# VectorE's order between the ranking and the second expert written out, and two GpSimd drains

## The chip, the cores and the metric

The kernel runs on one core of one Trainium2 chip. The metric is the device time of one execution in microseconds (us); the kernel before has a median of 478.66 us over three runs. In the profile TensorE is PE (its weight loads PEld), VectorE is DVE, ScalarE is ACT, GpSimd is POOL and SyncE is SP. A name with a q behind it (POOLq, SPq) is that engine's instruction queue: waits, register work, DMA issues, drains.

## The reference

Two stages follow each other. The first is block-sparse attention; the second sends each token of its output through one of eight experts, at most 80 tokens for each.

```python
# attention: q, k, v are (4, 8, 768, 64); blocks of 32; a row sees its neighbours,
# the first and the last block, and three sampled blocks
attn = softmax(where(mask, q @ k.T / 8, -1e9));  x = (attn @ v) as (3072, 512)
# experts: w_gate (512, 8), w1 (8, 512, 1024), w2 (8, 1024, 512), capacity 80
logits = x @ w_gate;  expert_idx = argmax(logits);  gate_w = softmax(logits)[expert_idx]
for e in range(8):
    tok_idx = the (at most) 80 tokens of expert e with the largest gate_w
    out[tok_idx] = gate_w[tok_idx, None] * (relu(x[tok_idx] @ w1[e]) @ w2[e])   # other rows stay 0
```

## The kernel before

**Attention** (0 to about 343 us of the profile) works through 24 groups: a block of 128 query rows of one batch, all heads. For each group DVE, ACT and POOL copy the visible keys together (`kx`, L237 on POOL), PE makes products (L363), transposes (L383) and the sums over values (L397). Each group has eight steps; `at(d, f)` queues `f` for d steps later. PE and SP follow this order as written; the other engines are ordered by the framework's planner, from its own estimates of durations. POOL also issues DMAs of its own: 32 loads of the first and last value blocks (`vw`, `vd`, L234), all in groups 0 to 13; later eight gathers of tokens and eight scatters of results. The last part of attention counts, for each token, how many of its expert's tokens rank above it; the ranking ends with `R` (L850) on DVE.

**The experts** start with `sl` (PE, L853), which turns the ranking into lists of token numbers and gates. DVE makes `toki`, the token numbers, from it (L858), and POOL gathers the tokens' rows, expert by expert (`xg`, L871). For expert e:

- `divide(e)`: DVE adds to the softmax sums and inverts them (`rs`, L925, L927); the rows are scaled into `xd` (L934), on DVE for e < 2 and on POOL from there on.
- `turn(e)`: PE transposes `xd` into `tx` (L944); `split_ps` cuts it into a high half on ACT (`xh`, L917) and a rest on DVE (`xl`, L918).
- `first_layer(e)`: 24 PE matmuls with w1 (`ph`, L958); `relu(e)` on ACT; `turn_h(e)` transposes and splits the result (`tq`, `hh`, `hl`); `second_layer(e)`: 24 matmuls with w2 (`po`, or `ph` for the last expert, L991); `finish(e)`: DVE multiplies by the gate (`ob`, L997) and POOL scatters the rows (L998).

Weights are float32 and are multiplied as two parts. Each expert has eight blocks of 128x1024 (four of w1, four of w2), loaded by SP (`raw`, L886) into a ring of 12 buffers. ACT casts a block into its high part (L895, L904) and DVE, or POOL for the fourth block of w2 of some experts, subtracts it for the rest (the `whl` rows of L896 and L911). I call this subtraction a **sub**. The parts lie in a ring of 11 pairs. SP issues its loads in order; a load waits until both cast and sub of the block that its buffer held are done, and so do all loads behind it.

Outside of attention the planner orders PE too. An order can be forced: what is traced inside `with tc.issue_after(ins)` stands behind `ins` if it runs on the same engine. In the kernel before a few such edges hold DVE: one sub of w1[0] behind the ranking, two behind `count_rounds`, the fourth behind `divide(0)`, and the subs of w1[1] and w2[0], `divide(e)` and `turn(e)` of later experts behind `xl` of the first; among these the planner chooses. The first expert's eight blocks are called w1[0] and w2[0] here, the second's w1[1] and w2[1].

After the last scatter all engines load a round count (L1057), skip a loop over further rounds (L1058) and end in a block of drains and barriers (L1114).

Of the kernel before, what the change touches and what calls it, by code (L numbers as in the profile page):

```python
# [24 lines left out]
P = 128  # L25
# [8 lines left out]
GATED, GLATE = range(0, 6), 4  # L34
NRQ = 4
BANKS = {(22, 4): "s", (23, 2): "t", (23, 3): "s", (23, 4): "t"}
SW1, SW2 = ("vvvp", "v"), ("v", "vvvp")
NEARLY = 2
FMID = 4
GACT = (23,)  # L40
NACC = {19: 2, 20: 2, 21: 2, 22: 4, 23: 3}
# [35 lines left out]
def kernel(  # L77
# [61 lines left out]
    with ExitStack() as actx:  # L139
# [427 lines left out]
        def at(delay, fn):  # L567
            queue.setdefault(stepno[0] + delay, []).append(fn)
# [143 lines left out]
        with tc.manual_schedule(engines={ENG.PE, ENG.SP}):  # L712

            def run(fs):
                for f in fs:
                    f()

            k0, k1 = load_k(0), load_k(1)
            run(k0[:1])
            load_full(0, k0[1:] + [lambda: load_q(0)])  # L720
            run(k1)
            load_rows(0)
            run(load_v(0))
            load_q(1)
            load_rows(1)
            load_q(2)
            nc.sync.dma_start(wg, w_gate.rearrange("(c p) e -> p c e", p=P))
            load_own()

            def globals_of(pair, b):  # L730
                with tc.issue_after(order["p"]):
                    load_v_global(pair % 2, b)

            for n, (j, b) in enumerate(ORDER):
                if n == 0:
# [12 lines left out]
                if n in FLOAD:  # L748
                    at(4, lambda n=n: load_full(FLOAD[n]))
                at(5, lambda n=n: load_q(n + 3))  # L750
                if n == 10:
                    at(0, lambda: run(load_k(2)))
                    at(6, lambda: run(load_k(3)))
                if n and n % 2 == 0 and n + 2 < len(ORDER):
                    def next_v(pair=n // 2 + 1):
                        run(load_v(pair))
                        load_rows(pair + 1)
                    at(6, next_v)
                    at(3, lambda pair=n // 2 + 1: spread_mask(pair))
# [72 lines left out]
    def moe_round(first):  # L832
        def after(ins):
            return tc.issue_after(ins) if first else nullcontext()
# [18 lines left out]
                mm = nc.tensor.matmul(sl[0:SLOT, 0:48], lhsT=R[:, :, t], rhs=tab[:, t].rearrange("p a e -> p (a e)"),  # L853
                                      start=(t == 0), stop=(t == NTILE - 1))
        warm(mm.ins, NWARM[1])
        toki = mp.tile([P, 2, NE], U32, name="toki")
        with nc.allow_low_precision(reason="sums of two whole numbers, each summed up in float32 before"):
            got = nc.vector.tensor_reduce(out=toki[0:SLOT, 0, :],  # L858
                                          in_=sl[0:SLOT, 0:2 * NE].rearrange("p (a e) -> p e a", a=2), axis=AX.X,
                                          op=ALU.add)  # L860
        sv = mp.tile([P, 6, NE], F32, name="sv")
        nc.vector.tensor_copy(sv[0:SLOT].rearrange("p a e -> p (a e)"), sl[0:SLOT, 0:48])
        tok = mp.tile([P, 2, NE], F32, name="tok")
        gate = mp.tile([P, NE], F32, name="gate")
        nc.vector.tensor_add(tok[0:SLOT, 0, :], sv[0:SLOT, 0, :], sv[0:SLOT, 1, :])
# [9 lines left out]
        for e in range(NG):  # L875
            gather(e)

        def load_w(e):
            if e >= NE:
# [28 lines left out]
        def split_lo(raw, done, ins):  # L908
            with after(ins):
                for t, (hi, lo) in zip(raw, done):  # L910
                    ins = nc.vector.tensor_sub(lo, t, hi.bitcast(F32))  # L911
            return ins.ins

        def split_ps(ps, name):
            hi = hpool.tile([P, ps.shape[-1]], F32R, name=name + "h")
# [79 lines left out]
        def finish(e):  # L995
            ob = hpool.tile([P, DM], F32, name="ob")
            nc.vector.tensor_scalar(ob[0:SLOT], outs[e][0:SLOT, :], gate[0:SLOT, e:e + 1], None, op0=ALU.mult)  # L997
            nc.gpsimd.indirect_dma_start(out=out[:, :],  # L998
                                         out_offset=bass.IndirectOffsetOnAxis(ap=toki[0:SLOT, 1, e:e + 1], axis=0),
                                         in_=ob[0:SLOT, :], in_offset=None, bounds_check=NT - 1, oob_is_err=False)  # L1000

        load_w(0)
        load_w(1)

        with after(order["act"]):
            w1h[0] = split_hi(w1s[0])
        split_lo(w1s[0][:1], w1h[0][:1], ranked.ins)
        nc.vector.tensor_scalar(tok[0:SLOT, 1, :], sv[0:SLOT, 5, :], -65536.0, 65536.0, op0=ALU.mult, op1=ALU.add)
        nc.vector.tensor_add(tok[0:SLOT, 1, :], tok[0:SLOT, 1, :], tok[0:SLOT, 0, :])
        nc.vector.tensor_copy(toki[0:SLOT, 1, :], tok[0:SLOT, 1, :])  # L1010
# [1 line left out]
        nc.vector.tensor_add(gate[0:SLOT], gate[0:SLOT], sv[0:SLOT, 4, :])  # L1012
        if first:
            with after(got.ins):
                counted = count_rounds()

        split_lo(w1s[0][1:3], w1h[0][1:3], counted.ins if first else None)
        for e in range(NE + 1):
            if e == 0:
                div = divide(0)  # L1020
                split_lo(w1s[0][3:], w1h[0][3:], div.ins)
                turned = turn(0)
                split0 = order["split"]
                warm(turned.ins, NWARM[2])
                if first:
                    with after(split0), after(order["hi"]):
                        w1h[1] = split_w(w1s[1][:NEARLY], SW1[0])
            if e + 1 < NE:
                with after(split0):
                    divide(e + 1)  # L1030
                turn(e + 1)
            if 0 < e < NE:
                turn_h(e - 1)
            if e < NE:
                first_layer(e)
            if e > 0:
                with after(order["act"]) if e == 1 else nullcontext(), after(split0) if e == 1 else nullcontext():
                    w2h[e - 1] = split_w(w2s[e - 1], SW2[min(e - 1, 1)])
# [8 lines left out]
            if e + 1 < NE:  # L1047
                if e == 0:
                    with after(order["act"]), after(split0):
                        w1h[1] = w1h.get(1, []) + split_w(w1s[1][len(w1h.get(1, [])):], SW1[0])  # L1050
                else:
                    w1h[e + 1] = split_w(w1s[e + 1], SW1[1])
            if e > 0:
                finish(e - 1)

# [62 lines left out]
```

## Time and profile before

| what | us |
|---|---|
| median of three runs (lowest, highest) | 478.66 (476.11, 479.69) |
| the profiled execution, its own time | 474.34 |
| its span in the trace | 472.5 |
| PE busy / DVE busy / ACT busy / POOL busy | 382.1 / 349.8 / 310.8 / 164.0 |

The time lies 1.84 us above the span. Instructions of the queues (waits, drains, DMA issues) are not counted as busy. The page's chain of waits shares the span out as PE 38%, DVE 20%, issue 13%, ACT 12%, DMA 11% and POOL 3%.

### The profile page before, as it was taken

Reading aid. Unit: us, or ns where it says so; the run is one execution under the profiler, and the core shown is the slowest. Engines: PE = TensorE matmul, PEld = TensorE weight load, DVE = VectorE, ACT = ScalarE, POOL = GpSimd, SP = SyncE. Lnnn points to the kernel's source line nnn. Section 1 sums busy time; section 2 is a strip of 40 time slices with the busy share of each in tenths; the row PEclk is TensorE's granted clock in tenths of the full one; section 3 lists DMA queues with packets and bytes.
Section 4 is the critical chain, followed back from the end, with each engine's and each line's share of the span. In section 5 each row is a group of like instructions: output and inputs, shape, how many; then the busy total and the mean of one; then the engine's idle time right before and its main releaser. Section 6 shows DMA issues by size and latency. Waiting matters only on the chain.

```text
span 472.5 us, 16982 instructions
## 1 busy us (share of the span) xinstructions
PE 382.1 (81%) x6294; PEld 266.7 (56%) x6296; DVE 349.8 (74%) x1366; ACT 310.8 (66%) x718; POOL 164.0 (35%) x422
## 2 busy tenths in 40 slices
PE   5826878798888889897988798867497999999990
PEld 2524655476666657675766576645364656665560
DVE  3752576687678798977999878757967899988920
ACT  2542677688568796786877656876755776787810
POOL 4540133243126363433333213141244354434320
PEclk9987899889999999999999998988558899999996
DMA  8999494979219999978669747892969695999400
GB/s 302 303 300 261 127 236 134 248 252 249 71 53 271 361 296 280 259 208 237 186 173 295 206 114 194 241 285 98 402 211 292 219 341 183 333 411 409 181 16 19
DMA packets 60779, 109.35 MB, mean 231 GB/s; under 512 B 6731, under 2 KB 19020, under 8 KB 60690
## 3 DMA queue, kind: packets, MB, share of 16 engines
q1 hardware_dynamic: 58130, 101.49, 69.1%
q0 software_dynamic: 2560, 6.71, 4.9%
q8 instruction: 52, 0.85, 0.8%
q14 instruction: 37, 0.30, 0.2%
HBM read 94.38 MB, written 13.99 MB: 229 GB/s over the span
## 4 chain that ended last, share of the span: by engine, by line
PE 38%; DVE 20%; issue 13%; ACT 12%; DMA 11%; POOL 3%; SPq 1%; ACTq 0%; DVEq 0%; POOLq 0%
PE S L363 9%; PE xb L397 7%; ACT sb L375 5%; PE ph L958 5%; DVE whl L896 4%; DVE dump L537 4%; PE pt L383 3%; DVE sb L371 3%; PE Sf L654 3%; DMA raw<-in_w_dram 3%; DMA vd<-in_v_dram 3%; DMA vw<-in_v_dram 2%; PE po L991 2%; ACT xs L598 2%; PE xb L674 1%
## 5 line engine op out<-in xcount | busy, mean ns | idle before, releaser
L375 ACT ACTIVATE sb<-sb,mn 128x256 f32<-128x256 f32 (+1 forms) x192 | 90.1, 503 | 42.0 <-DVE mn L371 39.1
L371 DVE CUSTOM_DVE_ANT_0 sb<-S,mask 128x256 f32<-128x256 f32 (+1 forms) x192 | 76.9, 422 | 50.0 <-PE S L363 36.3
L363 PE MATMUL S<-kx,qt 64*32 64x256 f32 x1408 | 71.1, 410 | 27.8 <-DMA qt<-in_qn_dram 8.7
L896 DVE TENSOR_TENSOR whl<-raw,whl 128x1024 fp32r<-128x1024 f32 x53 | 73.8, 1437 | 4.5 <-ACT whl L895 4.3
L363 PEld LDWEIGHTS S<-kx,qt 64*32 64x32 f32 x1408 | 37.4, 140 | 46.3 <-issue 27.1
L237 POOL COPY kx<-kt 128x128 f32 x88 | 30.4, 464 | 95.2 <-PE S L363 92.0
L895 ACT CAST whl<-raw 128x1024 fp32r<-128x1024 f32 x60 | 59.2, 1045 | 5.3 <-DMA raw<-in_w_dram 2.8
L397 PE MATMUL xb<-vw,pts 128*32 128x65 f32 x1408 | 53.7, 231 | 8.6 <-ACT pts L349 5.3
L397 PE MATMUL xb<-vd,pts 128*32 128x65 f32 x1408 | 53.8, 227 | 4.4 <-issue 4.2
L383 PE MATMUL pt<-ident,sb 128*128 128x128 f32 (+1 forms) x384 | 51.0, 277 | 4.2 <-ACT pts L349 3.4
L397 PEld LDWEIGHTS xb<-vw,pts 128*32 128x32 f32 x1408 | 37.5, 114 | 19.6 <-ACT pts L349 9.1
L958 PE MATMUL ph<-whl,xh 128*80 128x512 f32 x128 | 43.5, 410 | 3.6 <-DVE whl L896 3.5
L383 PEld LDWEIGHTS pt<-ident,sb 128*128 128x128 f32 (+1 forms) x384 | 41.1, 146 | 7.6 <-ACT pts L349 3.6
L397 PEld LDWEIGHTS xb<-vd,pts 128*32 128x32 f32 x1408 | 41.5, 114 | 5.3 <-issue 5.2
L285 ACT COPY kx<-kt 128x128 f32 x88 | 31.4, 438 | 10.3 <-PE S L363 10.3
L991 PE MATMUL po<-whl,hh 128*80 128x512 f32 x112 | 36.5, 395 | 0.0
L537 DVE TENSOR_SCALAR_CACHE_REDUCE dump<-keyrow,keycol,cnt 128x640 bf16<-128x640 f32 (+5 forms) x36 | 32.5, 904 | 1.1
L351 DVE COPY pts<-pt 128x512 f32<-128x512 f32 (+1 forms) x48 | 30.7, 640 | 3.5 <-PE pt L383 2.7
L661 ACT ACTIVATE sbf<-sbf,mn 128x768 f32<-128x768 f32 x16 | 15.0, 936 | 24.0 <-DVE mn L660 23.4
L285 DVE COPY kx<-kt 128x128 f32 x88 | 24.6, 315 | 8.0 <-PE S L363 7.9
L654 PE MATMUL Sf<-kt,qfull 128*128 128x512 f32 (+1 forms) x64 | 26.6, 540 | 4.8 <-DMA qfull<-in_qf_dram 3.3
L598 ACT COPY xs<-xb 128x260 f32<-128x260 f32 (+2 forms) x64 | 23.4, 366 | 10.5 <-PE xb L397 10.0
(211 smaller groups left out, 778.0 us busy)
## 6 DMA issues: line engine op xcount, KB each, us to landing
raw<-in_w_dram SPq DMA_DIRECT2D x64, 512.0 KB, 7.1
vw<-in_v_dram SPq DMA_DIRECT2D x44, 390.0 KB, 7.2
vd<-in_v_dram SPq DMA_DIRECT2D x132, 130.0 KB, 5.0
vf<-in_v_dram SPq DMA_DIRECT2D x24, 260.0 KB, 5.8
x_dram<-xs SPq DMA_DIRECT2D x24, 260.0 KB, 4.4
kt<-in_kT_dram SPq DMA_DIRECT2D x8, 768.0 KB, 7.2
qt<-in_qn_dram SPq DMA_DIRECT2D x24, 256.0 KB, 3.0
out_dram<-zero SPq DMA_DIRECT2D x12, 512.0 KB, 6.2
```

Source lines behind the costliest of these rows:

```text
L285: eng(far_keys(t, hps, k, r), KT[b][:, hps, bass.ds(vals[qbs[k], r] * BLK, BLK)])
L363: nc.tensor.matmul(banks[h][BLK * k:BLK * k + BLK, i].rearrange("p (g a) c -> p g (a c)", g=2), lhsT=QT[b, j][d, hp, :, k], rhs=keys, star ...
L371: ins = nc.vector.tensor_tensor_reduce(out=sb, in0=st, in1=masks[n // 2 % 2][0:r].rearrange("p g (a c) -> p (g a) c", a=4), scale=-0.125, ...
L375: order["s"] = nc.scalar.activation(p, p, AF.Exp, bias=mn, scale=-1.0).ins
L383: nc.tensor.transpose(pt[:, (2 * i + c) * r:(2 * i + c + 1) * r], p[:, c * P:(c + 1) * P], ident[0:r, 0:r])
L397: nc.tensor.matmul(xb[place:place + 32, o:o + 65], lhsT=pts[:, c * r + BLK * k:c * r + BLK * k + BLK], rhs=(vw, vd)[c][s][:, k, xb_b, hd * ...
L537: cmp = nc.vector.tensor_scalar(d, keyrow[:, lo * P:hi * P], key, c, op0=ALU.is_le, op1=ALU.add, accum_out=c)
L654: nc.tensor.matmul(st, lhsT=q[:, hp, :], rhs=KT[b][:, hp, part], start=True, stop=True)
L895: nc.scalar.copy(hi, t)
L896: eng.tensor_sub(lo, t, hi.bitcast(F32))
L958: nc.tensor.matmul(ps[0:SLOT, :], lhsT=l[:, cs], rhs=r[:, ws], start=(i == 0), stop=(i == 3 * HP - 1))
L991: nc.tensor.matmul(po[0:SLOT, :], lhsT=l[:, cs], rhs=r[:, ws], start=(i == 0), stop=(i == 23))
```

## The change

DVE's order from the ranking to the subs of w2[0] is written out, by a chain of edges (`order["dve"]`): three subs of w1[0]; `toki` and the small operations on lists and gates up to `count_rounds`; the fourth sub of w1[0] and the first of w1[1]; `divide(0)`; the second sub of w1[1]; `xl` of expert 0; the third sub of w1[1]; `divide(1)`; the fourth; `xl` of expert 1; three subs of w2[0]; from there on the planner chooses again. ACT casts w1[0], w1[1] and three blocks of w2[0] in one go. The gathers are traced behind the first three subs. The second part adds two drains on POOL: one in group 16 of attention, behind the last `kx` copy traced until then, and one behind the scatter of expert 5, the sixth.

```diff
-SW1, SW2 = ("vvvp", "v"), ("v", "vvvp")
-NEARLY = 2
+SW1, SW2 = "v", "vvvp"
+DRAINED = (16, 5)
...
                 at(5, lambda n=n: load_q(n + 3))
+                if n == DRAINED[0]:
+                    def drained():
+                        with tc.issue_after(order["p"]):
+                            nc.gpsimd.drain()
+                    at(6, drained)
...
+            if e == DRAINED[1]:
+                with tc.issue_after(put.ins):
+                    nc.gpsimd.drain()
...
+        order["dve"] = ranked.ins
         with after(order["act"]):
-            w1h[0] = split_hi(w1s[0])
-        split_lo(w1s[0][:1], w1h[0][:1], ranked.ins)
+            w1h[0], w1h[1], w2h[0] = split_hi(w1s[0]), split_hi(w1s[1]), split_hi(w2s[0][:3])
+        split_lo(w1s[0][:3], w1h[0][:3])
+        # toki, sv, tok and the gathers stand here now
...
-                counted = count_rounds()
-
-        split_lo(w1s[0][1:3], w1h[0][1:3], counted.ins if first else None)
+                order["dve"] = count_rounds().ins
+
+        split_lo(w1s[0][3:], w1h[0][3:])
+        split_lo(w1s[1][:1], w1h[1][:1])
         for e in range(NE + 1):
             if e == 0:
-                div = divide(0)
-                split_lo(w1s[0][3:], w1h[0][3:], div.ins)
-                turned = turn(0)
-                split0 = order["split"]
+                with after(order["dve"]):
+                    order["dve"] = divide(0).ins
+                split_lo(w1s[1][1:2], w1h[1][1:2])
+                with after(order["dve"]):
+                    turned = turn(0)
+                order["dve"] = order["split"]
                 warm(turned.ins, NWARM[2])
-                if first:
-                    with after(split0), after(order["hi"]):
-                        w1h[1] = split_w(w1s[1][:NEARLY], SW1[0])
+                split_lo(w1s[1][2:3], w1h[1][2:3])
             if e + 1 < NE:
-                with after(split0):
-                    divide(e + 1)
-                turn(e + 1)
+                with after(order["dve"]) if e < 2 else nullcontext():
+                    ins = divide(e + 1).ins
+                if e == 0:
+                    order["dve"] = ins
+                    split_lo(w1s[1][3:], w1h[1][3:])
+                with after(order["dve"]) if e == 0 else nullcontext():
+                    turn(e + 1)
+                if e == 0:
+                    order["dve"] = order["split"]
+                    split_lo(w2s[0][:3], w2h[0])
```

`split_lo` now puts each sub behind `order["dve"]` and leaves itself there. The rest of w2[0] (one block) and the weights of the later experts are split where they were.

## Rows read from the trace of the kernel before

**Rows 1.** Busy time by stretch: start:end, length, busy us (instructions) of PE, PEld, DVE, ACT, POOL, granted clock, DMA share, GB/s.
```profile
343.50:376.00 32.50, 29.05 (x126) 18.72 (x126) 23.61 (x47) 18.33 (x25) 12.26 (x10) 0.76 0.75 228
376.00:405.00 29.00, 27.36 (x142) 17.68 (x140) 29.00 (x32) 20.01 (x27) 12.98 (x8) 1.00 0.79 273
405.00:443.60 38.60, 37.24 (x185) 23.95 (x183) 35.04 (x35) 32.46 (x45) 16.84 (x8) 1.00 0.98 378
```

**Rows 2.** DVE in order of time: start, us, instruction, idle before and its releaser.
```profile
343.43 1.22 DVE L911 TENSOR_TENSOR whl<-raw,whl 128x1024 fp32r<-128x1024 f32 x1
347.62 0.17 DVE L858 TENSOR_REDUCE toki<-pa 80x8 uint32<-80x16 f32 x1 [2.96 <-PE pa L853]
...
348.93 2.36 DVE L911 TENSOR_TENSOR whl<-raw,whl 128x1024 fp32r<-128x1024 f32 x2
...
356.58 0.24 DVE L925 TENSOR_SCALAR rs<-xg 80x8 f32<-80x8 f32 x1 [1.86 <-DMA xg<-x_dram,toki]
358.18 0.17 DVE L925 TENSOR_SCALAR rs<-xg 80x8 f32<-80x8 f32 x1 [1.36 <-DMA xg<-x_dram,toki]
358.26 3.48 DVE L896 TENSOR_TENSOR whl<-raw,whl 128x1024 fp32r<-128x1024 f32 x3
...
362.87 0.68 DVE L934 TENSOR_TENSOR xd<-xg,rs 80x512 f32<-80x512 f32 x1
```

**Rows 3.** PE in order of time, around the second expert's transposes and later.
```profile
359.93 0.44 PE L976 MATMUL tq<-ident,h 80*128 80x80 f32 x4
363.70 0.77 PE L944 MATMUL tx<-ident,xd 80*128 80x80 f32 x4 [3.33 <-DVE xd L934]
...
395.67 0.70 PE L958 MATMUL ph<-whl,xh 128*80 128x512 f32 x2 [0.83 <-DVE whl L896]
...
457.86 0.40 PE L991 MATMUL ph<-whl,xh 128*80 128x512 f32 x1
```

**Rows 4.** Busy time by stretch, behind that wait of PE.
```profile
363.70:369.40 5.70, 5.70 (x23) 4.09 (x24) 4.66 (x8) 2.12 (x4) 1.04 (x1) 0.52 0.55 184
```

**Rows 5.** SP's queue, 343 to 376: who waited for whom, us in total, times, longest.
```profile
SPq L886 <- DVE whl L896: 14.3, 5, 5.6
SPq L886 <- DVE whl L911: 13.2, 3, 7.5
```

**Rows 6.** ACT in order of time, the first expert's high half.
```profile
353.68 0.43 ACT L917 CAST xh<-tx 128x320 fp32r<-128x320 f32 x1 [5.79 <-issue]
```

**Rows 7.** Instructions of line 1114, the kernel's end: duration ns min/median/max, first and last start.
```profile
L1114 SPq DRAIN  x3: 7/7/13, 466.9 to 472.0; - x3
L1114 POOLq DRAIN  x3: 46/98/3991, 467.7 to 472.3; - x3
```

**Rows 8.** The same of line 1107, the kernel's start.
```profile
L1107 POOLq DRAIN  x1: 169/169/169, 0.4 to 0.4; - x1
```

**Rows 9.** DMAs that POOL issues: count, KB each, median us to landing.
```profile
vw<-in_v_dram POOLq DMA_DIRECT2D x16, 130.0 KB, 7.2
vd<-in_v_dram POOLq DMA_DIRECT2D x16, 130.0 KB, 6.6
...
xg<-x_dram,toki POOLq DMA_INDIRECT x8, 4.4
out_dram<-ob,toki POOLq DMA_INDIRECT x8, 4.6
```

**Rows 10.** POOL in order of time: group 16's idle time, the sixth scatter, the last sub.
```profile
221.17 0.29 POOL L206 COPY mask<-quad 128x128 f32<-128x128 f32 x1 [3.05 <-DVE mn L371]
...
445.72 1.65 POOL L998 DMA_INDIRECT out_dram<-ob,toki  x1 [3.16 <-DVE ob L997]
450.82 2.39 POOL L896 TENSOR_TENSOR whl<-raw,whl 128x1024 fp32r<-128x1024 f32 x1 [3.46 <-ACT whl L895]
...
461.84 0.91 POOL L998 DMA_INDIRECT out_dram<-ob,toki  x1 [4.60 <-DVE ob L997]
```

**Rows 11.** The scatters of line 998: issue to landing.
```profile
DMA to landing us min/median/max: 2.9/4.6/6.3
```

More of the change, by code (lines that the diff above doesn't have):

```diff
@@ L855, in moe_round @@
         warm(mm.ins, NWARM[1])
[L856 to L865, printed above, removed]
         xgs, xts, w1s, w2s, w1h, w2h, hs, outs = {}, {}, {}, {}, {}, {}, {}, {}
@@ L873, in gather @@
                 xgs[e] = xg
-        for e in range(NG):
-            gather(e)
         def load_w(e):
@@ L906, in split_hi, with split_lo @@
             return done
[L908 to L912, printed above, removed]
+        def split_lo(raw, done):
+            for t, (hi, lo) in zip(raw, done):
+                with after(order["dve"]):
+                    order["dve"] = nc.vector.tensor_sub(lo, t, hi.bitcast(F32)).ins
         def split_ps(ps, name):
@@ L997, in finish @@
             nc.vector.tensor_scalar(ob[0:SLOT], outs[e][0:SLOT, :], gate[0:SLOT, e:e + 1], None, op0=ALU.mult)
-            nc.gpsimd.indirect_dma_start(out=out[:, :],
-                                         out_offset=bass.IndirectOffsetOnAxis(ap=toki[0:SLOT, 1, e:e + 1], axis=0),
-                                         in_=ob[0:SLOT, :], in_offset=None, bounds_check=NT - 1, oob_is_err=False)
+            put = nc.gpsimd.indirect_dma_start(out=out[:, :],
+                                               out_offset=bass.IndirectOffsetOnAxis(ap=toki[0:SLOT, 1, e:e + 1], axis=0),
+                                               in_=ob[0:SLOT, :], in_offset=None, bounds_check=NT - 1, oob_is_err=False)
+            if e == DRAINED[1]:
+                with tc.issue_after(put.ins):
+                    nc.gpsimd.drain()
         load_w(0)
         load_w(1)
+        order["dve"] = ranked.ins
         with after(order["act"]):
-            w1h[0] = split_hi(w1s[0])
-        split_lo(w1s[0][:1], w1h[0][:1], ranked.ins)
+            w1h[0], w1h[1], w2h[0] = split_hi(w1s[0]), split_hi(w1s[1]), split_hi(w2s[0][:3])
+        split_lo(w1s[0][:3], w1h[0][:3])
+        toki = mp.tile([P, 2, NE], U32, name="toki")
+        with after(order["dve"]), nc.allow_low_precision(reason="sums of two whole numbers, each summed up in float32 before"):
+            got = nc.vector.tensor_reduce(out=toki[0:SLOT, 0, :],
+                                          in_=sl[0:SLOT, 0:2 * NE].rearrange("p (a e) -> p e a", a=2), axis=AX.X,
+                                          op=ALU.add)
+        sv = mp.tile([P, 6, NE], F32, name="sv")
+        nc.vector.tensor_copy(sv[0:SLOT].rearrange("p a e -> p (a e)"), sl[0:SLOT, 0:48])
+        tok = mp.tile([P, 2, NE], F32, name="tok")
+        gate = mp.tile([P, NE], F32, name="gate")
+        nc.vector.tensor_add(tok[0:SLOT, 0, :], sv[0:SLOT, 0, :], sv[0:SLOT, 1, :])
+        for e in range(NG):
+            gather(e)
         nc.vector.tensor_scalar(tok[0:SLOT, 1, :], sv[0:SLOT, 5, :], -65536.0, 65536.0, op0=ALU.mult, op1=ALU.add)
@@ L1014, in moe_round @@
             with after(got.ins):
[L1015 to L1017 removed]
+                order["dve"] = count_rounds().ins
+        split_lo(w1s[0][3:], w1h[0][3:])
+        split_lo(w1s[1][:1], w1h[1][:1])
         for e in range(NE + 1):
             if e == 0:
[L1020 to L1023 removed]
+                with after(order["dve"]):
+                    order["dve"] = divide(0).ins
+                split_lo(w1s[1][1:2], w1h[1][1:2])
+                with after(order["dve"]):
+                    turned = turn(0)
+                order["dve"] = order["split"]
                 warm(turned.ins, NWARM[2])
[L1025 to L1027 removed]
+                split_lo(w1s[1][2:3], w1h[1][2:3])
             if e + 1 < NE:
[L1029 to L1031 removed]
+                with after(order["dve"]) if e < 2 else nullcontext():
[8 more added lines that the diff above has]
+                    split_lo(w2s[0][:3], w2h[0])
             if 0 < e < NE:
@@ L1036, in moe_round @@
             if e > 0:
-                with after(order["act"]) if e == 1 else nullcontext(), after(split0) if e == 1 else nullcontext():
-                    w2h[e - 1] = split_w(w2s[e - 1], SW2[min(e - 1, 1)])
+                w2h[e - 1] = w2h.get(e - 1, []) + split_w(w2s[e - 1][len(w2h.get(e - 1, [])):], SW2 if e > 1 else "v")
                 if e == NE - 1:
@@ L1046, in moe_round @@
             load_w(e + 2)
[L1047 to L1052, printed above, removed]
+            if 0 < e < NE - 1:
+                w1h[e + 1] = split_w(w1s[e + 1], SW1)
             if e > 0:
```

## The prediction

> **What bounds the kernel now.** I read the stages first: the busy time by stretch [rows 1]. In the first expert's stretch (343.5 to 376) DVE is busy 23.61 of 32.50 us and nothing is full; from 376 to 405 DVE is busy 29.00 of 29.00; from 405 to 443.6 PE (37.24 of 38.60) and the DMA engines (0.98) are nearly full. So the time that DVE leaves empty in the first stretch is missing in the second, which is all DVE, and the third can only start as early as the second lets it.
>
> Then I read DVE's own order [rows 2] for what its empty time is. It waits 2.96 us for PE's lists, 1.86 us for the second expert's gathered rows, and 1.36 us for the third's. When the second expert's rows are there (356.58), DVE doesn't finish with them: a sum for the third expert and four subs go first (three of them in the row at 358.26), and `xd` of the second expert runs at 362.87 only. PE's order shows the bill [rows 3]: it finishes the first expert's first layer and half of its transposes at 360.37 (359.93 + 0.44) and stands still for 3.33 us until 363.70, on that `xd`. Behind this wait its granted clock is 0.52 for 5.70 us [rows 4], the lower level of 1.2 GHz; from 376 on it is 1.00 [rows 1].
>
> Last, the end of the kernel, which no view of the engines counts as busy: one of POOL's three drains in the closing block takes 3.99 us, where SP's take 0.007 to 0.013 [rows 7].
>
> **DVE's order, step by step.** *Subs into the wait for the lists.* A sub is 1.22 us; two more in front of `toki` are 2.44 us in a hole of 2.96 [rows 2], so `toki` still starts at 347.62. The two subs behind the counting (2.36 us) stay two, of other blocks: nothing.
>
> *The second expert.* One sub (1.22) goes into the hole of 1.86. Then, at 356.58, `divide(1)` runs through: 0.24 for the sum, some 0.2 for the reciprocal (an estimate; its tiles are as small as the sum's), 0.68 for `xd` [rows 2], ended at 357.7 where it ended at 363.55. The third expert's sum moves behind the subs of w2[0]; it feeds a division on POOL that is wanted an expert later.
>
> *PE.* With `xd` there at 357.7, the transposes can stand right behind the first layer, at 360.4, 3.3 us earlier. Before the second expert's matmuls can start, ACT's 0.43 us cast of `xh` [rows 6] follows, with a semaphore on either side: I allow 0.8 us of new waiting. A wait of 0.83 us at 395.67 [rows 3] lies in a stretch whose clock is 1.00 [rows 1], so I expect the clock to stay up too: 5.70 us at 0.52 are 2.96 at full clock, 2.7 less. PE is ahead by 3.3 + 2.7 - 0.8 = 5.2 us; without the new waiting, 6.0.
>
> *DVE.* It is ahead by the holes filled: 2.44 + 1.22 + 1.36 = 5.0 us. Against that stands a new wait: `xl` of expert 1 is now fixed in front of the subs of w2[0]. DVE reaches it at 357.7 + 1.22 = 358.9; with the transposes at 360.4 (0.77) and the cast it is ready at about 361.1 to 361.6 (363.70 to 364.9 before), so up to 2.2 us are lost if PE has them behind the whole first layer, none if PE takes them in between. DVE is ahead by 2.8 to 5.0 us.
>
> *What it is worth at the end.* The next stretch is DVE's alone, so DVE's lead, the smaller of the two, is what passes: I take the middle, 3.9 us. Behind it loads follow subs: SP's queue waited 14.3 and 13.2 us for subs in this stretch [rows 5], so with earlier subs buffers come free, and the stretch that the DMAs fill moves as a whole. Bounds: 6.0 us (PE's lead) and nothing (the rivals).
>
> *Other moves.* SP: loads into the buffers of w1[0] leave some 3 us earlier (two subs run before `toki` instead of behind the counting); those into w2[0]'s buffers, w1 of the third expert, wait for subs that ended from 359.5 on and now end from 360.1 to 362.8 on, 0.6 to 3.3 us later. They are hidden as long as w1[2] isn't needed before some 372. ACT: four more casts in one go before `xh` of expert 0, 3.9 to 4.2 us at a cast's 1 us, in an idle time of 5.79 [rows 6]: nothing; without that cover the first layer would start late by as much. POOL: the gathers still wait for `toki` alone. DVE's small operations on gates and output rows may slip behind subs; their first user is the first scatter, much later: nothing.
>
> **The two drains.** The question is what 3.99 us are spent on. All of POOL's own DMAs are in (the last scatter, at 461.84 [rows 10], lands after 2.9 to 6.3 us [rows 11], and POOL's closing code comes behind the wait for it), so it is not a transfer. Drains of the same engine with no DMA since the last one take 0.17 us at the kernel's start [rows 8] and 0.05 and 0.10 behind the long one [rows 7]. Between them POOL issued 16 + 16 + 8 + 8 = 48 DMAs [rows 9]. I take it that the drain works through what these left behind: 3.99 / 48 = 0.083 us for each (an estimate). The other end: 3.99 us is a fixed price for the last drain, and then nothing is saved.
>
> The Trainium skill (VectorE: DVE Perf Modes, The DRAIN you can't avoid) says that the drains around a kernel take a constant 12 ns on all five engines; by that there would be nothing to gain at the end, and the sum would lose this term. SP's rows agree with it, POOL's 3,991 ns does not, so the row decides. The Trainium skill (Perfetto Trace Analysis, Sequencer-only Instruction) also says that the profiled time of such an instruction leaves out its wait on semaphores; nothing here shows that by itself.
>
> By the estimate the drain in group 16 takes 32 x 0.083 = 2.7 us. POOL idles 3.05 us there before 221.17 [rows 10], so I cost it at nothing; where the planner puts it elsewhere, the copies of keys for the next group wait behind it, for at most 2.7 us (3.99 if the price is fixed). A gain there is excluded, as nobody waits for what it clears. The drain behind the sixth scatter (445.72) has to let that scatter land, a median 4.6 and at most 6.3 us [rows 11], and then 14 x 0.083 = 1.2 us: POOL is free between 451.5 and 453.2. The last sub on POOL, at 450.82 (2.39 us) [rows 10], ends at 455.6 at the latest; PE takes up the second half of the last w2 at 457.86 [rows 3]. Nothing lost. The last drain then has two scatters left: 0.17 us, to which I add 0.1 for the empty drain: it shortens by 3.7 us (bounds 0 and 3.9).
>
> **Sum.** 474.34 - 3.9 - 3.7 = 466.7 against the profiled execution. That execution is 4.3 us under the median of the runs, and I carry the difference over: 478.66 - 7.6 = **471.1 us**.
>
> **Rivals.** *A: the lead is spent.* DVE's new wait in front of `xl`, or the later loads of w1[2], eat DVE's holes; PE's earlier start ends in waits for subs from 376 on. For it: that stretch is DVE's to the last tenth. Against it: 2.44 us go into a hole that opens before any of this. Only the drain's gain is left: 478.66 - 3.7 = 475.0.
>
> *B: the last drain stays long.* Its price is fixed, or hangs on something that the earlier drains don't clear. For it: a single row. Against it: the three short drains. 478.66 - 3.9 = 474.8.
>
> *C: slower.* PE's order keeps the second expert's transposes where they were, at 363.70. Then DVE stands from 358.9 to 365 in front of `xl`, the subs of w2[0] end 7.2 us later than before (366.7 instead of 359.5), and SP's queue, in order, holds w1[2] and all behind it as long. It decides if the transposes come later than about 363. Price: up to 7.2 us, less the drain's 3.7: 482.2. Against it: their place at 363.70 follows `xd` at 362.87, which moves.
>
> *D: neither part does anything* (the holes are refilled by other waits, the drain stays): 478.7.
>
> **How the numbers follow.** Chances: forecast 0.64, A 0.14, B 0.10, C 0.06, D 0.06. The forecast's own range: its terms at their best, 478.66 - 6.0 - 3.9 = 468.8, and at 2.8 and 3.0, 472.9; the runs shown scatter 2.6 below and 1.0 above their median, so 466 to 474. The range has to take in A and B with that scatter, so it is 465.5 to 477; it leaves out C, D and a little at either end. About 1% (4.8 us) is what a measurement of this kernel tells from no change: faster means under 473.9. The forecast lies there but for a tail, A and B for a third each: 0.61 + 0.05 + 0.03 = 0.69. C counts half as slower by over 1% (above 483.4), with a tail of D: 0.05. The rest is 0.26.
>
> **What would show it.** In the trace after: DVE's hole before `toki` under 0.7 us; `xd` of expert 1 ended near 358; PE's wait before the second expert's transposes under 1 us and its granted clock 1.00 behind it; DVE full from about 372 on; PE's last matmul some 4 us earlier; POOL's last long drain near 0.3 us and two new drains of 2.7 and about 6 us (or 1.2, if the wait isn't counted). Wrong would be: a hole of over 2 us before `xl` of expert 1, PE waiting for w1[2], the last drain still near 4 us, or PE waiting for keys behind group 16.

## Result, and the profile after

The changed kernel takes **462.61 us** (median of six runs from 461.12 up) against 477.20 (six runs, 472.48 to 479.69) of the kernel before: a ratio of 0.9705, 95% interval 0.9641 to 0.9769. Runs in a slower state (here 469.00 and 582.68) count in a median but are left out of a ratio, here and in the table below. The prediction was 471.1, with a range from 465.5 to 477. The direction was right, the gain nearly twice as large as forecast, and the time lies below the range. Two later comparisons of the same pair gave 0.9715 (0.9661 to 0.9769) and 0.9765 (0.9707 to 0.9823), that is 14.6, 13.3 and 11.1 us between the medians.

The profiled execution took 463.06 us, with a span of 461.3. Its ranking ended at 343.16 where before it ended at 343.52, so nearly all of the 11.2 us of span lies behind the ranking, and the two traces can be laid side by side. First the stages, cut at the same distance from the ranking's end as in [rows 1], with the same columns:

```profile
343.14:375.64 32.50, 29.86 (x144) 18.58 (x144) 28.67 (x55) 21.07 (x28) 15.90 (x12) 0.87 0.84 278
375.64:404.64 29.00, 29.00 (x148) 19.31 (x147) 26.79 (x30) 20.78 (x29) 14.70 (x7) 1.00 0.88 302
404.64:443.24 38.60, 37.21 (x184) 24.18 (x183) 30.87 (x32) 31.45 (x41) 14.54 (x9) 1.00 0.87 314
```

In the first stretch DVE does 5.06 us more than before (28.67 against 23.61). In the second the roles have changed: PE is now the one that is busy throughout (29.00 of 29.00, before 27.36), and DVE, which was full, has 2.21 us to spare. DVE's own order, which answers to [rows 2]:

```profile
342.40 0.76 DVE L855 TENSOR_TENSOR R<-rankb,slots 128x480 bf16<-128x480 bf16 x2
343.07 3.49 DVE L903 TENSOR_TENSOR whl<-raw,whl 128x1024 fp32r<-128x1024 f32 x3
347.26 0.17 DVE L1006 TENSOR_REDUCE toki<-pa 80x8 uint32<-80x16 f32 x1 [0.69 <-PE pa L858]
...
348.57 2.36 DVE L903 TENSOR_TENSOR whl<-raw,whl 128x1024 fp32r<-128x1024 f32 x2
353.71 0.17 DVE L916 TENSOR_SCALAR rs<-xg 80x8 f32<-80x8 f32 x1 [2.78 <-DMA xg<-x_dram,toki]
...
357.49 0.16 DVE L916 TENSOR_SCALAR rs<-xg 80x8 f32<-80x8 f32 x1
...
357.92 0.69 DVE L925 TENSOR_TENSOR xd<-xg,rs 80x512 f32<-80x512 f32 x1
```

The hole before `toki` is 0.69 us (before 2.96), and the second expert's `xd` runs at 357.92 instead of 362.87. What was not foreseen stands at 353.71: the first expert's rows are late, DVE waits 2.78 us for them. PE, as in [rows 3], and then the 5.70 us behind the second expert's transposes, as in [rows 4]:

```profile
354.66 0.65 PE L935 MATMUL tx<-ident,xd 80*128 80x80 f32 x4 [1.85 <-issue]
...
355.87 0.68 PE L949 MATMUL ph<-whl,xh 128*80 128x512 f32 x2
...
358.75 0.47 PE L935 MATMUL tx<-ident,xd 80*128 80x80 f32 x4 [0.43 <-DVE xd L925]
...
438.15 0.46 PE L949 MATMUL ph<-whl,xh 128*80 128x512 f32 x1 [0.81 <-ACT whl L887]
439.41 0.69 PE L949 MATMUL ph<-whl,xh 128*80 128x512 f32 x2 [0.58 <-DVE whl L888]
...
453.87 0.39 PE L982 MATMUL ph<-whl,xh 128*80 128x512 f32 x1
```

```profile
358.75:364.45 5.70, 5.70 (x33) 3.80 (x34) 5.60 (x9) 3.29 (x6) 3.12 (x3) 1.00 0.77 227
```

PE's wait is 0.43 us (before 3.33), its granted clock behind it 1.00, the upper level of 2.4 GHz (before 0.52). The last matmul ends at 454.26; before, the row at 460.38, 0.39 us long, ended at 460.77.

Last, the end: duration in ns as minimum, median and maximum, then first and last start. After:

```profile
L1125 POOLq DRAIN  x3: 52/98/217, 460.2 to 461.0; - x3
...
L1069 POOLq INC_SWDGE_SEM  x1: 231/231/231, 458.3 to 458.3; - x1
...
L994 POOLq DRAIN  x1: 6012/6012/6012, 440.6 to 440.6; - x1
...
L754 POOLq DRAIN  x1: 3712/3712/3712, 218.8 to 218.8; - x1
```

and one line of the kernel before that the prediction did not read:

```profile
L1058 POOLq INC_SWDGE_SEM  x1: 1160/1160/1160, 464.8 to 464.8; - x1
```

The longest closing drain is 0.217 us instead of 3.991 [rows 7]. A step of POOL's queue on the semaphores of its own DMAs, ahead of it, also shrank, from 1.160 to 0.231. From the last matmul to the end it is now 7.0 us, before 11.8: 4.8 less, of which these two are 3.77 + 0.93.

### The profile page after: what moved, and what is told of

Its sections match the earlier page's. It is cut to its first block, busy times and chain, and to the rows that moved or that the text cites. A ratio compares the mean times of both kernels' runs of the same rounds, so it can differ in the third digit from the quotient of the medians.

```text
span 461.3 us, 16972 instructions
## 1 busy us (share of the span) xinstructions
PE 378.3 (82%) x6294; PEld 264.7 (57%) x6296; DVE 344.8 (75%) x1366; ACT 310.5 (67%) x718; POOL 168.9 (37%) x422
## 5 line engine op out<-in xcount | busy, mean ns | idle before, releaser
L888 DVE TENSOR_TENSOR whl<-raw,whl 128x1024 fp32r<-128x1024 f32 x46 | 59.3, 1338 | 9.7 <-ACT whl L887 9.4
L887 ACT CAST whl<-raw 128x1024 fp32r<-128x1024 f32 x53 | 52.6, 1045 | 15.5 <-DMA raw<-in_w_dram 15.3
L383 PE MATMUL pt<-ident,sb 128*128 128x128 f32 (+1 forms) x384 | 49.5, 272 | 3.9 <-ACT pts L349 3.4
L383 PEld LDWEIGHTS pt<-ident,sb 128*128 128x128 f32 (+1 forms) x384 | 40.1, 143 | 6.8 <-ACT pts L349 3.6
L949 PE MATMUL ph<-whl,xh 128*80 128x512 f32 x128 | 42.0, 398 | 1.5 <-ACT whl L887 0.8
L285 ACT COPY kx<-kt 128x128 f32 x88 | 31.2, 435 | 10.9 <-PE S L363 10.9
L888 POOL TENSOR_TENSOR whl<-raw,whl 128x1024 fp32r<-128x1024 f32 x7 | 20.8, 2974 | 44.8 <-ACT whl L887 42.4
L598 ACT COPY xs<-xb 128x260 f32<-128x260 f32 (+2 forms) x64 | 23.4, 366 | 11.8 <-PE xb L397 11.3
L484 POOL TENSOR_SCALAR tab<-oh_all 128x8 bf16<-128x8 f32 x23 | 10.2, 444 | 57.5 <-DVE oh_all L468 43.7
## 6 DMA issues: line engine op xcount, KB each, us to landing
kt<-in_kT_dram SPq DMA_DIRECT2D x8, 768.0 KB, 10.9
```

Source lines behind the costliest of these rows:

```text
L285: eng(far_keys(t, hps, k, r), KT[b][:, hps, bass.ds(vals[qbs[k], r] * BLK, BLK)])
L383: nc.tensor.transpose(pt[:, (2 * i + c) * r:(2 * i + c + 1) * r], p[:, c * P:(c + 1) * P], ident[0:r, 0:r])
L888: eng.tensor_sub(lo, t, hi.bitcast(F32))
L949: nc.tensor.matmul(ps[0:SLOT, :], lhsT=l[:, cs], rhs=r[:, ws], start=(i == 0), stop=(i == 3 * HP - 1))
```

## The experiments

Two lengths are read from every trace: **A**, from the end of the ranking to the end of PE's last matmul, and **B**, from there to the end of the span. For the kernel after A is 454.26 - 343.16 = 111.1 and B 461.3 - 454.3 = 7.0. But for the early drain, the orders of all kernels are the same up to the ranking, yet it ended between 341.6 and 350.8 us; A and B are free of that scatter, the medians are not. Each group of experiments ran beside the kernel before, whose medians were 478.27, 477.53, 477.20 and 476.07.

| run | ranking ends | A | B | median | ratio (interval) |
|---|---|---|---|---|---|
| before | 343.5 | 117.2 | 11.8 | 477.20 | |
| e4, before again | 346.3 | 117.2 | 11.8 | 478.91 | 1.004 (1.000 to 1.008) |
| after | 343.2 | 111.1 | 7.0 | 462.61 | 0.9705 (0.9641 to 0.9769) |
| e10, after again | 344.6 | 110.2 | 7.0 | 464.25 | 0.9715 (0.9661 to 0.9769) |
| e13, after again | 348.2 | 110.8 | 7.0 | 465.02 | 0.9765 (0.9707 to 0.9823) |
| e1, order alone | 348.9 | 112.5 | 11.7 | 473.53 | 0.9829 (0.9752 to 0.9907) |
| e2, drains alone | 347.0 | 116.5 | 7.1 | 471.98 | 0.9882 (0.9823 to 0.9941) |
| e3, after, late drain only | 344.9 | 111.3 | 7.0 | 465.54 | 0.9735 (0.9673 to 0.9798) |
| e14, the same again | 343.3 | 111.4 | 7.0 | 463.29 | 0.9703 (0.9634 to 0.9772) |
| e5, after, early drain only | 350.8 | 111.7 | 8.4 | 466.44 | 0.9756 (0.9696 to 0.9815) |
| e15, before, early drain only | 341.6 | 117.7 | 8.5 | 474.30 | 0.9976 (0.9940 to 1.0012) |
| e6, loads held | 342.9 | 111.9 | 7.0 | 467.59 | 0.9784 (0.9734 to 0.9834) |
| e7, second expert free | 344.3 | 116.6 | 7.1 | 470.06 | 0.9851 (0.9812 to 0.9891) |
| e8, hole open | 342.2 | 118.6 | 7.1 | 472.22 | 0.9894 (0.9844 to 0.9944) |
| e9, nothing of DVE's on POOL | 349.0 | 111.0 | 7.0 | 467.89 | 0.9696 (0.9626 to 0.9766) |
| e12, no subs on POOL | 346.2 | 109.5 | 7.0 | 464.50 | 0.9749 (0.9675 to 0.9824) |

**The two parts, each alone.** e1 is the kernel after without drains, e2 the kernel before with both:

```diff
-DRAINED = (16, 5)
+DRAINED = (99, 99)
```

> The changed kernel without its two drains. Theory (two gains that add: DVE's order moves PE's last matmul, 460.77 to 454.25 in the two traces; the drains shorten what follows it, 11.77 to 7.05 us): PE's last matmul stays near 454.3, the end behind it is 11.8 us again with a closing POOL drain of about 4.0 us, and the time is 4.7 us above the changed kernel's, about 467.3. Rival (the drains also steady or speed the experts, or the order alone gives more than the traces say): PE's last matmul moves by over 1 us, or the time is outside 466 to 469.

> The kernel before with the two drains and nothing else. Theory: PE's last matmul near 460.8, closing POOL drain 0.2 us, 7.1 us behind the last matmul, time 4.7 us below the kernel before. Rival (the group 16 drain costs attention time, or the drain behind the sixth scatter delays the last experts): the attention part ends over 0.5 us later than 343.4, or the gain is under 3.5 us.

The order shortens A (to 112.5) and leaves B; the drains shorten B (to 7.1) and leave A within 0.7 us. The closing drain is the drains' doing alone: 3.991 us in e1, 0.212 in e2. The two parts nearly add up: A and B together gain 4.8 us in e1 and 5.4 in e2, against 10.9 to 11.8 with both. The rest has a place. In e1, as in e5, which also has the new order without the late drain, POOL's last sub runs beside three of DVE's, which then take 5.69 us, and PE waits 0.69 us for DVE behind them:

```profile
451.21 3.11 POOL L888 TENSOR_TENSOR whl<-raw,whl 128x1024 fp32r<-128x1024 f32 x1 [0.63 <-ACT whl L887]
```

```profile
449.72 5.69 DVE L888 TENSOR_TENSOR whl<-raw,whl 128x1024 fp32r<-128x1024 f32 x3
```

With the late drain that sub of POOL's waits for the drain and starts when DVE's subs are all but done (446.84 in the kernel after, where they end at 446.98), and no trace with it has this wait. Two expectations missed: e1's median of 473.53 lies outside the 466 to 469 that its theory gave, and e2 gained 6.3 us in the median, not 4.7.

**Which drain.** e3 keeps the late one only (`DRAINED = (99, 5)`), e5 the early one only (`(16, 99)`).

> The changed kernel with the drain behind the sixth scatter alone. Theory (0.083 us for each DMA issued since the last drain): that drain clears 46 DMAs instead of 14, so it is 2.7 us longer than the 6.01 us of the changed kernel, the closing drain stays at 0.2 us, and POOL's last subtraction starts up to 2.7 us later (449.5 instead of 446.8); PE needs it at about 453, so the time is that of the changed kernel within 0.5 us. Rival (a drain has a fixed price of near 4 us, whatever it clears): the drain's length stays near 6.0 us.

> The changed kernel with the drain in group 16 alone. Theory (a price per DMA of POOL): the closing drain clears 16 DMAs and takes 16 x 0.083 + 0.1 = 1.4 us; its time lies 1.2 to 2.0 us above the changed kernel's (the other queue instruction that shrank with it, 1.16 to 0.23 us, may stay at some 0.5). Rival (a fixed price while anything is left): the closing drain takes 3.7 to 4.0 us.

With the late drain alone B is the same 7.0. Its own length is 7.55 us in e3 and 7.57 in e14, where the kernel after has 6.01; that is 1.5 more for 32 DMAs more, and not the 2.7 expected. With the early drain alone the closing drain is 1.367 us in e5, and the same in e15:

```profile
L1120 POOLq DRAIN  x3: 52/98/1367, 465.6 to 467.5; - x3
...
L1064 POOLq INC_SWDGE_SEM  x1: 511/511/511, 463.4 to 463.4; - x1
```

That gives three points: 48 DMAs left, 3.991; 16 left, 1.367; 2 left, 0.217. Per DMA this is (3.991 - 1.367) / 32 = 0.082 and (1.367 - 0.217) / 14 = 0.082 us. The step on the semaphores follows the same count: (1.160 - 0.511) / 32 = 0.020 and (0.511 - 0.231) / 14 = 0.020. So the price of the end is what POOL's DMAs left since its last drain, and the drain behind the sixth scatter clears all but the two scatters behind it; the one in group 16 is not needed.

The drains in the middle fit the same price once the end of what stands in front of them is looked up. In the kernel after, the copies in front of the early drain end at 219.77, and the drain, recorded from 218.78 on, ends 2.72 us behind them; the same interval is 2.71 or 2.72 in all eleven traces with this drain, and 32 x 0.082 is 2.62:

```profile
218.43 1.34 POOL L237 COPY kx<-kt 128x128 f32 x4 [3.86 <-PE S L363]
222.58 0.55 POOL L206 COPY mask<-quad 128x128 f32<-128x128 f32 x1 [2.80 <-DVE ltsum L470]
```

The late drain ends 3.84 us behind the instruction that issues the sixth scatter in e3 and e14, with 46 DMAs to clear (46 x 0.082 = 3.77), but still 2.29 behind it in the kernel after, with 14 (1.15). There the scatter's landing decides: in e10, the same kernel, it lands at 446.53 and the drain ends at 447.15, 0.6 us behind it, as in e2, e8, e9 and e12.

**The kernel before, again**, as a measure of what means nothing:

> The kernel before, unchanged, for a second trace and for the spread of its times. The two traces differ by 11.2 us, the medians by 14.6. Theory (the rest is this kernel's own spread: its executions run from 472.5 to 479.7, and the one profiled was a quick one): the executions spread over more than 4 us again, and a slower trace loses its time in one place, either in attention or behind the wait of PE at 360. Rival (the changed kernel really gains 14.6 us everywhere): the executions agree within 2 us at about 477.

A and B come out the same to 0.1 us. The ratio is 1.004, with an interval just above 1 for the very same kernel: 0.4% between medians is not to be read as a difference here.

**Loads held.** After's three early subs free three buffers of w1[0] at once; e6 takes other blocks first, so that SP's loads leave later:

```diff
-        split_lo(w1s[0][:3], w1h[0][:3])
+        split_lo([w1s[0][i] for i in (0, 2, 3)], [w1h[0][i] for i in (0, 2, 3)])
...
-        split_lo(w1s[0][3:], w1h[0][3:])
+        split_lo(w1s[0][1:2], w1h[0][1:2])
```

> The changed kernel with one swap: the second block of w1[0] is subtracted behind the counting and the fourth in front of the lists, so SP's load into the second block's buffer, and all loads behind it, leave about 2.5 us later. In the changed kernel DVE waits 2.78 us for the first gathered rows (0.68 before) and they come 5.3 us after POOL starts that gather (3.2 before). Theory (the freed loads take the DMA engines, at 401 GB/s from 348 to 350 us, from the gather): the rows come 3.2 to 3.6 us after the start, and PE's first layer starts 10.7 to 11.2 us behind the ranking instead of 12.7; PE's last matmul 109.4 to 110 us behind it, 1.1 to 1.7 less. Rival (the gather is late for another reason, DVE's subtractions beside POOL's descriptor writing): 12.7 us again.

The first expert's first layer starts 10.6 us behind the ranking, as before the change (354.16 - 343.52 = 10.6), and not 12.7 as in the kernel after. As many subs run in front of the lists as before this swap, so the rival, DVE's subs beside POOL, falls, and the late rows of the first expert are the loads' doing. But A is 111.9, no better, where 109.4 to 110 was expected, and PE's order shows why:

```profile
353.46 0.69 PE L949 MATMUL ph<-whl,xh 128*80 128x512 f32 x2
...
358.51 0.47 PE L935 MATMUL tx<-ident,xd 80*128 80x80 f32 x4 [2.59 <-DVE xd L925]
```

```profile
351.28 0.17 DVE L916 TENSOR_SCALAR rs<-xg 80x8 f32<-80x8 f32 x1 [0.69 <-DMA xg<-x_dram,toki]
...
357.24 0.17 DVE L916 TENSOR_SCALAR rs<-xg 80x8 f32<-80x8 f32 x1 [2.09 <-DMA xg<-x_dram,toki]
```

The first gather now lands early, and the second is the late one: DVE waits 2.09 us for it and PE 2.59 for DVE. This wait was not followed by a lower clock. The stretch behind it, with the columns of [rows 1], reads 1.00, where the one behind 3.33 us in the kernel before read 0.52 [rows 4]:

```profile
358.51:364.21 5.70, 5.70 (x33) 3.80 (x34) 5.60 (x9) 3.30 (x6) 1.67 (x2) 1.00 1.07 270
```

**Either half of the order.** e7 leaves the hole filled and gives the second expert's division back to the planner; e8 keeps that division early and leaves the hole open.

```diff
 # e7
-                with after(order["dve"]) if e < 2 else nullcontext():
-                    ins = divide(e + 1).ins
+                with after(split0):
+                    divide(e + 1)
...
 # e8
-        split_lo(w1s[0][:3], w1h[0][:3])
+        split_lo(w1s[0][:1], w1h[0][:1])
...
-        split_lo(w1s[0][3:], w1h[0][3:])
-        split_lo(w1s[1][:1], w1h[1][:1])
+        split_lo(w1s[0][1:3], w1h[0][1:3])
...
```

> The kernel after, but VectorE's order is fixed only up to the first expert's xl: the second expert's division, its xl and the subs behind it are left to the planner, as before the change. All numbers are PE's last matmul counted from the end of the ranking (before 117.2, after 110.2 to 111.1 us), which is free of attention's own scatter. Theory 1 (the second expert's early division is what pays, since PE waited for it and fell to the lower clock): 115 to 117, PE's wait of over 3 us before the second expert's transposes back; median some 468. Theory 2 (the subs in the hole before the lists pay, the division's place does not): 111 to 112.5, median as after. Half from each: 113 to 114.5.

> The kernel after, but with one sub in front of the lists' reduction where after has three; the other two run behind the counting and push later subs behind the second expert's division, which stays early. Theory 1 (the early division pays; the hole's 2.44 us on VectorE are only a lead that PE does not need, being full from the second expert on): PE's last matmul 110 to 112.5 us behind the ranking. Theory 2 (VectorE's lead is what passes): 2.4 us of it missing, 113 to 114.5. As the loads into w1[0]'s buffers leave later, the first gather should land some 1.5 us sooner behind its issue (4 us instead of 5) in both.

A is 116.6 in e7 and 118.6 in e8 (before 117.2): neither half has any of the gain to speak of, and e8 lies outside of what either theory gave it. In e7 two subs go ahead of the second expert's `xd`, as before the change:

```profile
359.89 0.17 DVE L916 TENSOR_SCALAR rs<-xg 80x8 f32<-80x8 f32 x1 [1.53 <-DMA xg<-x_dram,toki]
359.97 1.21 DVE L903 TENSOR_TENSOR whl<-raw,whl 128x1024 fp32r<-128x1024 f32 x1
361.11 0.19 DVE L918 RECIPROCAL rs<-rs 80x8 f32<-80x8 f32 x1
361.22 1.17 DVE L903 TENSOR_TENSOR whl<-raw,whl 128x1024 fp32r<-128x1024 f32 x1
362.31 0.68 DVE L925 TENSOR_TENSOR xd<-xg,rs 80x512 f32<-80x512 f32 x1
```

That is the value of 116.6 which the early division's theory wanted, but not its path. PE's wait there is 0.74 us only; the first gather landed still later (PE waited 2.40 us for it), and waits of 0.6 to 1.1 us come back further on. In e8 PE is early at first, and then stands still for the fourth expert's rows, whose division on POOL takes 4.13 us:

```profile
364.81 1.04 POOL L925 TENSOR_TENSOR xd<-xg,rs 80x512 f32<-80x512 f32 x1 [4.49 <-DVE rs L918]
371.06 4.13 POOL L925 TENSOR_TENSOR xd<-xg,rs 80x512 f32<-80x512 f32 x1 [5.20 <-issue]
```

```profile
364.95 1.99 DVE L888 TENSOR_TENSOR whl<-raw,whl 128x1024 fp32r<-128x1024 f32 x1
...
370.74 0.19 DVE L918 RECIPROCAL rs<-rs 80x8 f32<-80x8 f32 x1
370.85 3.44 DVE L888 TENSOR_TENSOR whl<-raw,whl 128x1024 fp32r<-128x1024 f32 x3
```

```profile
375.25 0.50 PE L935 MATMUL tx<-ident,xd 80*128 80x80 f32 x4 [2.63 <-POOL xd L925]
```

```profile
375.25:381.00 5.75, 5.75 (x27) 3.83 (x28) 2.80 (x8) 1.41 (x4) 5.56 (x4) 0.70 0.68 249
404.00:411.00 7.00, 5.00 (x15) 2.96 (x15) 5.84 (x7) 2.72 (x4) 1.96 (x2) 0.76 0.98 348
```

The planner put the reciprocal for it (370.74) behind subs, and POOL's division then ran beside three more of them: 4.13 us for what took 1.04 at 364.81. At 364.81 POOL had started first, and the sub beside it took 1.99; at 371.06 a sub was already running, and the three took 3.44 together, their usual time. The Trainium skill (GPSIMD Engine Reference, Specifications) says that POOL shares its SBUF interfaces with DVE and contends with DVE instructions that read two SBUF inputs; these rows agree. PE waits 2.63 us, then 2.00 us until 406.16 for a sub, and behind each wait its granted clock is 0.70 and 0.76 where it is 1.00 in the kernel after. So e8 does not weigh DVE's 2.44 us by themselves: it shows how a small shift turned into two waits of PE's, each paid twice here, once in the wait and once in the clock.

**Is DVE still the bound?** e9 gives DVE all divisions and all subs (`NDV = 8`, `SW2 = "v"`), e12 the subs only (`SW2 = "v"`).

> The changed kernel with all divisions and all subtractions on DVE, none on POOL. In the traces a subtraction of DVE that runs beside one of POOL takes up to 3.43 us instead of 1.21, and beside POOL's divisions 2.07. Theory (each engine slows the other): no subtraction of DVE over 1.4 us once the gathers are out, and DVE's busy time behind the ranking falls in spite of 6 more divisions (0.68 each) and 7 more subtractions (1.21 each). The time: PE is without a wait from 365 to 437 us in the changed kernel, so at most its last waits (0.81 + 0.58) go: 0 to 1.4 us less. Rival (the slow subtractions come from elsewhere, such as the DMA writes): they stay, and DVE, with more work, makes PE wait: 2 us or more slower.

> The kernel after, but with every sub of the second layers' weights on VectorE (after gives one block in four from the third expert on to POOL); the divisions from the third expert on stay on POOL. Theory 1 (PE is the bound from the second expert on; VectorE's subs stretched beside POOL's no longer matter): PE's last matmul 109.5 to 111 us behind the ranking, at most the two waits of 0.81 and 0.58 us at 437 to 439 gone, median within 1% of after. Theory 2 (VectorE is still the bound, and POOL beside it costs it time): 3 us less or more, 107 to 108 if the stretching was the cost, 113 or more if the added 1.2 us for each block is.

e12's PE ends earliest of all, 109.5 us behind the ranking, with seven subs more on DVE. Its stretches from 15 us behind the ranking on:

```profile
361.17:378.17 17.00, 16.43 (x85) 10.70 (x86) 16.81 (x26) 12.37 (x17) 9.41 (x6) 1.00 0.87 282
378.17:408.17 30.00, 30.00 (x155) 20.02 (x154) 29.16 (x34) 22.76 (x32) 16.20 (x6) 1.00 0.92 320
408.17:444.17 36.00, 35.63 (x178) 23.44 (x177) 32.31 (x35) 29.16 (x39) 12.14 (x4) 1.00 0.92 322
```

From 378 to 408 PE is full, and DVE, with 29.16 of 30.00, doesn't hold it up. In e9 no sub of DVE's takes over 1.23 us, as expected, but DVE's busy time behind the ranking rose (97.1 us over 118) where it was to fall. A is 111.0, with one wait of 1.85 us for a division that DVE does behind subs. e12's median of 464.50 lies among the three of the kernel after, so it is no measurably better version.

**Does the early drain shorten attention?** This was the last candidate for the part of the medians that A and B leave over.

> The kernel after once more, in more rounds, as the partner of the next two. By the traces its part behind the ranking is 118 us against 129 of before. If attention is the same in both, the medians differ by 11 us (ratio 0.977); if attention gains too, by 13 to 14.6 as in the earlier runs (0.970 to 0.973).

> The kernel after without the drain in group 16. If that drain shortens attention, this median is 1.5 to 3 us above the one of the kernel after; if attention only scatters, within 1 us of it.

> The kernel before with the drain in group 16 alone, no drain behind a scatter. The closing drain then has 16 DMAs left: 1.37 us instead of 3.99, and the step on semaphores behind it 0.51 instead of 1.16, so 3.3 us less at the end (ratio 0.993). If the drain shortens attention as well, 4.8 to 6.3 us less (0.987 to 0.990).

It does not: without it e14 is 1.7 us below e13. e15 gains 0.24%, with an interval that takes in none and 0.6%, and so less than the 0.7% that its shorter end alone was expected to give; its trace has that shorter end (B is 8.5) and no shorter A (117.7).

## Why the prediction missed

**The places were right.** The hole before `toki` (0.69, said under 0.7), the second expert's `xd` (ended at 358.6, said near 358), PE's wait and clock behind it (0.43 and 1.00), the closing drain (0.217, said near 0.3): all as said. PE took the second expert's transposes in between the first layer's matmuls, at 358.75, so rival C had no ground, and no wait stands in front of the second `xl`. Rival B fell by the three points on one line, rival A by PE's 29.00 of 29.00, and D with both. One sign failed, DVE full from about 372 on: it was busy 26.79 of 29.00 us from 375.64.

**The step that failed** is "DVE's lead, the smaller of the two, is what passes: I take the middle, 3.9 us". A fell by 6.1 to 7.1 us in the three traces of the kernel after, which is PE's lead, forecast at 5.2 to 6.0, and a little more. DVE's lead did come out near its forecast. Its last sub ends 107.3 us behind the ranking before (first row below) and 103.8 after (second row), 3.4 earlier; in e10 and e13 it is 4.4 and 3.7 earlier:

```profile
447.30 3.48 DVE L896 TENSOR_TENSOR whl<-raw,whl 128x1024 fp32r<-128x1024 f32 x3
```

```profile
441.15 5.83 DVE L888 TENSOR_TENSOR whl<-raw,whl 128x1024 fp32r<-128x1024 f32 x4
```

But it was not what passed: PE's last matmul moved by more than DVE's last sub. DVE's full stretch from 376 to 405 was read as the bound, although PE was busy 27.36 of its 29.00 us as well [rows 1].

That DVE's own lead came out near 3.9 is luck, since its path was another. DVE's full stretch was also taken for a fixed amount of work, and it was not. Over the 118 us behind the ranking the three traces read, before, after and e12 (columns as in [rows 1]):

```profile
343.52:461.52 118.00, 110.32 (x523) 70.56 (x522) 97.14 (x122) 76.48 (x102) 47.03 (x28) 0.93 0.73 257
```

```profile
343.16:461.16 118.00, 107.06 (x523) 69.04 (x522) 92.34 (x123) 76.20 (x102) 50.50 (x29) 0.95 0.75 258
```

```profile
346.17:464.17 118.00, 106.17 (x523) 68.99 (x522) 97.54 (x129) 76.28 (x102) 47.80 (x22) 0.95 0.75 257
```

In the kernel after DVE is busy 4.8 us less for the same instructions. Up to its last sub it is also idle no less than before (13.8 us, before 12.5), so on balance its lead did not come from filled holes. The subs are where the busy time went: the 57 that DVE does behind the ranking add up to 81.03 us before and 74.94 after (in e4 and e10, the same two kernels again, to 81.17 and 74.65). Ten of the 57 take over 1.5 us before, five after, the longest 3.4 in both, and each of these has an instruction of POOL beside it. With no sub on POOL, in e12, the longest is 2.11, and with no division either, in e9, 1.23. So the new order moves subs out of POOL's way, which no step of the prediction had. It is not needed for the gain, though: in e12 DVE is busy 97.54 us, as long as before, and A is 109.5. That PE and no longer DVE holds the stretch is what the 29.00 of 29.00 and e12's 30.00 of 30.00 show.

By parts, from the traces: the wait for `xd` 2.9 less (3.33 to 0.43), the clock behind it 2.7, the later waits of over 0.4 us 1.5 (0.58 + 0.83 + 1.03 + 0.42 before, 0.81 + 0.58 after), and against them the first layer 2.1 later. That is 5.0 of 6.1. The rest is 0.4 us in shorter waits and 0.7 in PE's busy time, which from the first layer on falls by 3.48 us (99.80 to 96.32, 476 matmuls each), 0.7 more than the clock's part; why is open. The parts are a tally and not separate savings: in e4 the lower clock costs only 1.7 us (a granted clock of 0.70 in the 5.70 us from 366.76), and A is 117.2 all the same.

**A cost that was missed** is "loads into the buffers of w1[0] leave some 3 us earlier", put down at nothing. The second and the third of them left 4.4 us earlier, 2.3 and 3.4 us behind the ranking. The first gather was issued with those loads in flight (the DMAs moved 400 GB/s from 348 to 350, before none), and the first layer began 2.1 us later against the ranking. e6 shows the cause, and also that removing it buys nothing, since the second gather is late instead.

**A slip in the sum.** An `xl` that is ready at 361.6 where DVE is there at 358.9 costs 2.7 us and not 2.2, so DVE's lead had to start from 2.3 and not from 2.8. Nothing came of it, as the wait didn't occur.

**The drains** were right in mechanism: 0.083 us for each DMA was predicted, 0.082 measured. Missed was the 0.93 us of the step on semaphores, so the end gained 4.8 and not 3.7. The early drain's record is 3.71 us long and not 2.7, because it starts 1.0 us before the copies in front of it end; behind them it takes the 2.7. POOL's next copy starts 2.80 us behind those copies, before 3.05, so the idle time covers it. The Trainium skill's constant 12 ns (VectorE: DVE Perf Modes, The DRAIN you can't avoid) is off for POOL here even at its shortest, 46 ns [rows 7].

**Sum.** Forecast 3.9 + 3.7 = 7.6; in the traces 6.1 + 4.8 = 10.9. With 10.9 the prediction's own base gives 478.66 - 10.9 = 467.8, inside its range. Of the other 5.2 us to 462.61, 1.5 are the base, the median of three runs, where six gave 477.20. The remaining 3.7 no experiment could put down to the change. The comparisons gave 14.6, 13.3 and 11.1 us; A and B together give 129.0 - 118.1, 117.2 and 117.8, that is 10.9, 11.8 and 11.2, so the third comparison is covered whole, the second but for 1.5, and the first is the one out of line. e10's median, 464.25, came out below the 465 to 469 that A and B were expected to give. Attention isn't shown to gain: over all 16 traces the ranking ends at 341.6 to 347.0 us in the four with the old order and at 342.2 to 350.8 in the twelve with the new one. Why it moves so much under the same order stays open.

## What to carry over

An engine that is full in a stretch need not be the bound: here PE was nearly full beside it, and its lead passed. When instructions are stretched by a neighbour, look at the spread of their durations before taking an engine's busy time for fixed. A wait of PE's can cost the clock behind it as well as its length (it did behind 3.33 and 2.63 us, it did not behind 2.59 in e6), so an order that avoids several waits at once can be worth more than its halves, which here gave next to nothing each. A drain of POOL's DMAs placed while POOL has nothing to do takes that work out of the kernel's end.

## What was not expected of the hardware

The end pays for each of POOL's DMAs twice, 0.082 us in the drain and 0.020 in the step on semaphores. The same division on POOL took 1.04 us where it started ahead of a sub of DVE's, which then took 1.99, and 4.13 where it came behind one. A drain's record can start before the instruction that it is traced behind: the late drain starts at 440.65, its scatter is issued from 442.64 to 444.36, and the drain ends at 446.66. So of its 6.01 us 3.7 pass before the scatter is issued; the last sub on POOL followed at 446.84 without harm.
